# Zero packets of 14 KiB instead of 8 KiB beside the loads and stores of an attention backward kernel

## The chip, the cores and the metric

One core of one Trainium2 chip runs the whole program. The metric is the device time of one execution in microseconds, lower is better. Most executions of a kernel lie within 0.3%, but some runs of the kernel before lie near 800 us (791.42 to 800.26 over 20 runs), so medians and the ratios below differ by a few tenths of a per cent. In what follows PE is the matrix engine, DVE the vector engine and ACT the scalar engine; SBUF is the main memory on the chip, PSUM the one that receives the sums of the PE.

## The reference

One decoder step for two sequences and its gradients: layer norm, attention of 32 query heads (8 key/value heads, 128 wide) over the last 4,096 of 32,768 cached positions, a GeGLU feed-forward block, and the gradients of everything, bf16.

```python
W = min(4096, max(256, Sk // 4))                       # 4096 of 32768
k = jnp.repeat(k_cache[:, :, Sk - W:, :], rep, axis=1)  # v likewise
p = softmax(q k^T * Dh ** -0.5)
h = x + (p v) @ wo ;  h2 = h + (gelu(ln(h) @ w_gate) * (ln(h) @ w_up)) @ w_down
# outputs: h2 and the gradients of x, k_cache, v_cache, wq, wo, w_gate, w_up, w_down
```

The gradients of the two caches are full size. Outside the window they are zero, so 32 regions of 7.34 MB, 235 MB in all, are only zeros to be written. The rest is 49 MB read and 47 MB written.

## The kernel before

Zeros are written by GpSimd DMAs that read a small row of zero bytes again and again and cast each byte to four: a 2 KiB source row gives an 8 KiB packet. The loads and stores go through SyncE's queue. In the profile, q0 is the zeros and q1 the loads and stores.

```python
ZE = 2048
zt = const.tile([P, ZE], U8)                     # zero bytes
ZPK = Z * DH // 2 // ZE                          # 896 packets in a region
ZERO_PARTS = {i: ((4, 1), (15, 2), (2, 2), (15, 42), (12, 3), (P, 1), (16, 4)) for i in (30,)}
def zero_cast(i):                                # (rows, packets per row)
    dst, done = zero_regions[i].bitcast(F32), 0
    for rows, n in ZERO_PARTS.get(i, ((P, ZPK // P),)):
        src = zt[0:rows * (P // rows):P // rows, :]
        nc.gpsimd.dma_start(out=dst[done * ZE:(done + rows * n) * ZE]..., in_=src.unsqueeze(1).to_broadcast([rows, n, ZE]))
        done += rows * n
# ... all 32 are issued at the start and run, in order, whenever the DMA engines have room
```

Region 30 is cut so that transfers of 15 rows leave one DMA engine out. The computation is a chain: attention of batch 0, its middle part, score gradients, the same for batch 1, weight gradients, and a last stage of four jobs that write 8.4 MB of dK or dV each.

```python
def softmax(g):                                  # cut
    ef = stA.tile([P, NJ, REP], F32, tag="ef", name="ef", bufs=1)
    nc.vector.tensor_tensor(out=ef[:], in0=S[:], in1=negm..., op=ALU.add)
    nc.scalar.activation(out=ef[:], in_=ef[:], func=ACT.Exp)
    # ... three DVE reads of ef: ee, eT, lsum

for n, (b, what) in enumerate(jobs):             # last stage, cut
    rhs_bd = nxt
    for gq in range(2):
        # 16 x (2 matmuls, 2 evacuations) into two staging buffers of 16 KiB
        for a in range(2):
            for b2 in range(2):
                nc.sync.dma_start(out=dst_v[:, b, gq * 4 + a * 2 + b2, :, :], in_=sts[a][:, b2, :, :])   # 1 MiB
        if gq == 0 and n + 1 < len(jobs):
            nxt = bd_of(n + 1)                   # its scratch row lies inside staging buffer 1
```

Of the kernel before, what the change touches and what calls it, by code (L numbers as in the profile page):

```python
# [7 lines left out]
BF16 = mybir.dt.bfloat16  # L8
F32 = mybir.dt.float32
U8 = mybir.dt.uint8  # L10
U32 = mybir.dt.uint32
ACT = mybir.ActivationFunctionType
ALU = mybir.AluOpType
AX = mybir.AxisListType
PSUM = bass.MemoryType.PSUM

P = 128
B, D = 2, 512
HQ, HKV, REP, DH = 32, 8, 4, 128
W = 4096  # L20
NJ = W // P
# [6 lines left out]
NOR = (HQ * DH) // P  # L28
SCALE = DH ** -0.5
# [39 lines left out]
def kernel(ctx, tc, A_x, A_k_cache, A_v_cache, A_wq, A_wo, B_x, B_w_gate, B_w_up, B_w_down, grad_out,  # L69
                out_0, out_1, out_2, out_3, out_4, out_5, out_6, out_7, out_8):  # L70
    nc = tc.nc
# [4 lines left out]
    small = ctx.enter_context(tc.tile_pool(name="small", bufs=1))  # L76
# [12 lines left out]
    def evac(out, in_):  # L89
        if evac_i[0] % 2 == 0:  # L90
            nc.vector.tensor_copy(out=out, in_=in_)  # L91
        else:
            nc.scalar.copy(out=out, in_=in_)  # L93
        evac_i[0] += 1
# [3 lines left out]
    dKv = out_2[:, :, Z:, :].rearrange("b g (p j) d -> p b g j d", p=P)  # L98
    dVv = out_3[:, :, Z:, :].rearrange("b g (p j) d -> p b g j d", p=P)

    ZE = 2048
    zt = const.tile([P, ZE], U8)
    zero_regions = [o[b, g, 0:Z, :].rearrange("r d -> (r d)") for o in (out_2, out_3) for b in range(B) for g in range(HKV)]

    ZPK = Z * DH // 2 // ZE

    ZERO_PARTS = {i: ((4, 1), (15, 2), (2, 2), (15, 42), (12, 3), (P, 1), (16, 4)) for i in (30,)}

    def zero_cast(i):
        dst, done = zero_regions[i].bitcast(F32), 0  # L110
        for rows, n in ZERO_PARTS.get(i, ((P, ZPK // P),)):
            src = zt[0:rows * (P // rows):P // rows, :]
            nc.gpsimd.dma_start(out=dst[done * ZE:(done + rows * n) * ZE].rearrange("(p k e) -> p k e", p=rows, k=n),  # L113
                                in_=src.unsqueeze(1).to_broadcast([rows, n, ZE]))
            done += rows * n
# [23 lines left out]
    def load_v(b, g):  # L139
        Vt[b, g] = at(OFF_V + g * 8 * KIB, [P, NJ, DH], BF16, f"V{b}_{g}")  # L140
        nc.sync.dma_start(out=Vt[b, g][:], in_=Vv[:, b, g, :, :])
# [140 lines left out]
    rLb = small.tile([P, HQ], F32)  # L282
    rl = small.tile([P, 1], F32)
    dqT_bf = small.tile([P, NBH], BF16)
    dqT_hb = small.tile([P, HQ, B], BF16)
    dact = small.tile([P, NFR * B], F32)
    M_sb = at(OFF_M, [P, HQ, DH], BF16, "M")
    E = [at(OFF_E[b], [P, 8, 4, HQ], BF16, f"e{b}") for b in range(B)]
# [3 lines left out]
    def prefetch(b, g):  # L292
        if b == 0:
            if g == 0:
# [3 lines left out]
                for i in range(1, 4):  # L298
                    load_k(0, i)
                    load_v(0, i)  # L300
                nc.gpsimd.tensor_scalar(out=zt[:], in0=wq_sb[:, 0, 0:ZE // 2].bitcast(U8),
                                        scalar1=0, scalar2=None, op0=ALU.mult)
# [31 lines left out]
    def attention(b):  # L334
        with tc.tile_pool(name="ps_KT", bufs=2, space=PSUM) as ps_KT, \
# [41 lines left out]
            def softmax(g):  # L377
                S = S_ps.pop(g)
                mx = stA.tile([P, REP], F32, tag="mx", name="mx")
                nc.vector.reduce_max(out=mx[:], in_=S[:].rearrange("p j h -> p h j"), axis=AX.X)  # L380
                mT_ps = ps_A.tile([REP, P], F32, tag="st", name="mT_ps")
                nc.tensor.transpose(out=mT_ps[:], in_=mx[:], identity=ident_f32[:])
                mT = stA.tile([REP, 1], F32, tag="mT", name="mT")
                nc.vector.reduce_max(out=mT[:], in_=mT_ps[:], axis=AX.X)
                md = stA.tile([REP, REP], F32, tag="md", name="md")
                nc.vector.tensor_scalar(out=md[:], in0=ident_f32[0:REP, 0:REP], scalar1=mT[:, 0:1], scalar2=-1.0,
                                        op0=ALU.mult, op1=ALU.mult)
                negm_ps = ps_A.tile([P, REP], F32, tag="st", name="negm_ps")
                nc.tensor.matmul(out=negm_ps[:], lhsT=ones_f32[0:REP, 0:1].to_broadcast([REP, P]), rhs=md[:], start=True, stop=True)
                negm = stA.tile([P, REP], F32, tag="negm", name="negm")  # L390
                nc.vector.tensor_copy(out=negm[:], in_=negm_ps[:])
                ef = stA.tile([P, NJ, REP], F32, tag="ef", name="ef", bufs=1)
                ee = stA.tile([P, NJ, REP, 2], BF16, tag="ee", name="ee")
                nc.vector.tensor_tensor(out=ef[:], in0=S[:], in1=negm[:].unsqueeze(1).to_broadcast([P, NJ, REP]), op=ALU.add)
                nc.scalar.activation(out=ef[:], in_=ef[:], func=ACT.Exp)
                nc.vector.tensor_copy(out=ee[:], in_=ef[:].unsqueeze(3).to_broadcast([P, NJ, REP, 2]))
                Ef[g] = ee
                nc.vector.tensor_copy(out=eT[:].rearrange("p j a q -> p a j q")[:, :, :, g * REP:(g + 1) * REP],
                                      in_=ef[:].rearrange("p (a j) i -> p a j i", a=4))
                nc.vector.reduce_sum(out=lsum[:, 0, g * REP:(g + 1) * REP], in_=ef[:].rearrange("p j h -> p h j"), axis=AX.X)  # L400
# [102 lines left out]
    def middle(b):  # L503
        h0 = b * HQ
        with tc.tile_pool(name="ps_W", bufs=2, space=PSUM) as ps_W, \
             tc.tile_pool(name="ps_B", bufs=1, space=PSUM) as ps_B:
            attn_ps = ps_B.tile([B, D], F32)
            nc.tensor.matmul(out=attn_ps[:], lhsT=ident_bf[32:32 + B, 32:32 + B], rhs=x_32, start=True, stop=False)
            o_sel = at(OFF_KT + 3 * KIB, [P, HQ, 4], BF16, f"o_sel{b}")
# [67 lines left out]
            dhT = transpose_rows(ps_B.tile([P, NDR, B], BF16, tag="sm", name="psT_dh"), dh_bf, f"dh{b}", strided=False, p0=64)  # L577

            dO2_ps = ps_B.tile([P, NOR, B], F32, tag="da", name="dO2_ps")
            dO2 = small.tile([P, NOR], F32, name=f"dO2_{b}", tag="dO2")  # L580
            NPE = 16
            dhB_ps = ps_B.tile([P, D], F32, tag="gu", name="dhB_ps")
            nc.tensor.matmul(out=dhB_ps[:], lhsT=ident_bf[64:64 + B, 64 + b:65 + b].to_broadcast([B, P]), rhs=dh_bf, start=True, stop=True)
# [28 lines left out]
            dqM_ps = ps_B.tile([P, HQ], F32, tag="gu", name="dqM_ps")  # L612
            for q in range(HQ):
                nc.tensor.matmul(out=dqM_ps[:, q:q + 1], lhsT=M_sb[:, q, :], rhs=dOT_bf[:, h0 + q:h0 + q + 1], start=True, stop=True)
            dq_f32 = small.tile([P, HQ], F32, name=f"dq_f32_{b}", tag="dq_f32")
            nc.vector.tensor_tensor(out=dq_f32[:], in0=dqM_ps[:], in1=rLb[:], op=ALU.mult)
            nc.vector.tensor_tensor(out=dq_f32[:], in0=dq_f32[:], in1=pkT[:], op=ALU.subtract)
            nc.vector.tensor_scalar(out=dqT_bf[:, h0:h0 + HQ], in0=dq_f32[:], scalar1=SCALE, scalar2=None, op0=ALU.mult)
            nc.scalar.activation(out=dqT_hb[:, :, b], in_=dq_f32[:], func=ACT.Copy, scale=SCALE)
            if b == 1:  # L620
                ffn_ps = ps_B.tile([B, D], F32, tag="tmp", name="ffn_ps")
                for k in range(NFR):
# [61 lines left out]
    with tc.tile_pool(name="ps_G", bufs=2, space=PSUM) as ps_G:  # L684
# [36 lines left out]
        for (r0, nr) in ((0, 14), (14, 14), (28, 4)):  # L721
            add_group([D] * nr, lambda k, r0=r0: Ro_flat[:, (r0 + k)::NOR], lambda k: DH_bf[:],
                      lambda st, r0=r0, nr=nr: nc.sync.dma_start(out=gwo_v[:, r0:r0 + nr, :],
                                                                 in_=st[:, :nr * D].rearrange("p (a n) -> p a n", n=D)))
# [34 lines left out]
    with tc.tile_pool(name="ps_W2", bufs=2, space=PSUM) as ps_W, \  # L759
         tc.tile_pool(name="ps_G4", bufs=2, space=PSUM) as ps_G, \  # L760
         tc.tile_pool(name="ps_Q", bufs=1, space=PSUM) as ps_Q:
        dq_ps = ps_Q.tile([NBH, DH], BF16, tag="x")
        nc.tensor.transpose(out=dq_ps[:], in_=dqT_bf[:], identity=ident_bf[:])
        dq_bhd = at(OFF_BHD, [NBH, DH], BF16, "dq_bhd")
        nc.vector.tensor_copy(out=dq_bhd[:], in_=dq_ps[:])
        build_R(dq_bhd)
        d_ln1_ps = ps_Q.tile([B, NDR, P], F32)

        def use_q(h, wqT_h):
            nc.tensor.matmul(out=d_ln1_ps[:].rearrange("b a p -> b (a p)"), lhsT=dqT_hb[:, h, :],  # L770
                             rhs=wqT_h[:].rearrange("d a p -> d (a p)"), start=(h == 0), stop=(h == HQ - 1))
        pipelined(HQ, lambda h: tblock(ps_W, lambda r: wq_sb[:, r, h * DH:(h + 1) * DH]), use_q, depth=2)
        ln1 = at(OFF_R1, [B, D], F32, "ln1")
        nc.vector.tensor_scalar(out=ln1[:], in0=x_bf[:], scalar1=mv1[:, 0:1], scalar2=rstd1[:, 0:1],
                                op0=ALU.subtract, op1=ALU.mult)
        nc.vector.tensor_copy(out=ln2_bf[:], in_=ln1[:])
        dx = at(OFF_FROW, [B, D], F32, "dx")
        ln_bwd(d_ln1_ps[:].rearrange("b a p -> b p a"), ln1[:], rstd1, dh[:], "1", dx, at(OFF_FROW + 2 * KIB, [B, D], F32, "tmp"))
        nc.vector.tensor_copy(out=dh_bf, in_=dx[:])
        nc.sync.dma_start(out=out_1.rearrange("b s d -> (b s) d"), in_=dh_bf)  # L780

        L_ps = ps_Q.tile([NBH, D], F32, tag="x")
        nc.tensor.matmul(out=L_ps[:], lhsT=selB, rhs=ln2_bf[:], start=True, stop=True)
        L_bf = at(OFF_L, [NBH, D], BF16, "L")
        nc.vector.tensor_copy(out=L_bf[:], in_=L_ps[:])
        gwq_v = out_4.rearrange("(p r) n -> p r n", r=NDR)
        for r in range(NDR):
            st = at(OFF_WQ + r * 8 * KIB, [P, HQ * DH], BF16, "gq")
            for c4 in range(4):
                ps = ps_G.tile([P, 1024], F32, tag="ps_g", name="ps_gq")  # L790
                for q in range(2):
                    col0 = c4 * 1024 + q * 512
                    nc.tensor.matmul(out=ps[:, q * 512:(q + 1) * 512], lhsT=L_bf[:, r::NDR],  # L793
                                     rhs=Ro_flat[:, col0:col0 + 512], start=True, stop=True)
                evac(st[:, c4 * 1024:(c4 + 1) * 1024], ps[:])
            nc.sync.dma_start(out=gwq_v[:, r, :], in_=st[:])
# [63 lines left out]
```

## Time and profile before

| | before |
|---|---|
| time, median of 20 runs | 792.5 us |
| profiled span | 790.7 us |
| PE, DVE, ACT busy | 72%, 60%, 36% |
| DMA moved | 332.4 MB, 420 GB/s over the span |
| end of attention of batch 1 | 398.7 us |
| last zero packet | 768.5 us |
| R: the fourth job's operand can be built | 750.6 us |

The page cuts the span into 40 slices; a row of 40 rates tells at once whether DMA ever rests. A kernel with one resource that never rests is read from the bytes; only where the row sags does the chain of waits set the time. The moments in the table are starts of single instructions in the trace. "Last zero packet" is by the trace's own zero point; with the packet records lined up by their last end it is 769.8.

### The profile page before, as it was taken

Reading aid. Unit: us, or ns where it says so; the run is one execution under the profiler, and the core shown is the slowest. Engines: PE = TensorE matmul, PEld = TensorE weight load, DVE = VectorE, ACT = ScalarE, POOL = GpSimd, SP = SyncE. Lnnn points to the kernel's source line nnn. Section 1 sums busy time; section 2 is a strip of 40 time slices with the busy share of each in tenths; the row PEclk is TensorE's granted clock in tenths of the full one; section 3 lists DMA queues with packets and bytes.
Section 4 is the critical chain, followed back from the end, with each engine's and each line's share of the span. In section 5 each row is a group of like instructions: output and inputs, shape, how many; then the busy total and the mean of one; then the engine's idle time right before and its main releaser. Section 6 shows DMA issues by size and latency. Waiting matters only on the chain. (4 is left out here: it accounts for less than half of the span.)

```text
span 790.7 us, 12452 instructions
## 1 busy us (share of the span) xinstructions
PE 569.7 (72%) x5096; PEld 303.4 (38%) x5096; DVE 473.8 (60%) x1161; ACT 281.0 (36%) x406; POOL 40.6 (5%) x58
## 2 busy tenths in 40 slices
PE   3899998787687989840937968989697842783072
PEld 3656564445565555420515444534242210220020
DVE  2599999127533989760731386765636953993093
ACT  1434330134345333100201343644444540683062
POOL 4300000000000000000000000000000000000000
PEclk9799999867698999885867868965587685897586
DMA  8999999999999999999999999999999999999998
GB/s 366 418 418 422 419 426 427 423 429 428 427 421 420 425 425 423 426 424 431 427 430 429 428 426 428 428 423 428 434 421 430 423 420 422 424 420 422 422 377 362
DMA packets 40986, 332.44 MB, mean 420 GB/s; under 512 B 2000, under 2 KB 2016, under 8 KB 2144
## 3 DMA queue, kind: packets, MB, share of 16 engines
q0 software_dynamic: 29376, 234.88, 77.7%
q1 hardware_dynamic: 11540, 96.75, 48.9%
q8 instruction: 40, 0.66, 0.3%
q14 instruction: 18, 0.15, 0.0%
q10 hardware_dynamic: 12, 0.01, 0.0%
HBM read 49.30 MB, written 282.33 MB: 419 GB/s over the span
## 5 line engine op out<-in xcount | busy, mean ns | idle before, releaser
L408 DVE TENSOR_TENSOR mem<-mem,ee 128x512 bf16<-128x512 bf16 x512 | 180.9, 416 | 39.9 <-PE M_ps L419 39.9
L419 PE MATMUL M_ps<-mem 128*128 128x512 bf16 x512 | 141.8, 395 | 6.5 <-DVE mem L408 6.2
L93 ACT CAST mem<-ps_g 128x512 bf16<-128x512 f32 x128 | 74.3, 587 | 86.1 <-PE ps_g L822 80.7
L822 PE MATMUL ps_g<-mem 128*128 128x512 bf16 x256 | 82.5, 417 | 20.1 <-DVE mem L91 13.7
L366 ACT COPY mem<-KT_ps 128x1024 bf16<-128x1024 bf16 x64 | 63.1, 1013 | 82.2 <-PE KT_ps L364 77.4
L91 DVE CAST mem<-ps_g 128x512 bf16<-128x512 f32 x128 | 82.6, 688 | 7.1 <-ACT mem L93 3.5
L364 PE MATMUL KT_ps<-ident_bf,mem 128*128 128x128 bf16 x512 | 46.3, 235 | 30.5 <-DMA mem<-in_A_k_cache_dram 25.6
L113 POOL DMA_DIRECT2D out_dram<-zt x38 | 32.5, 998 | 670.7 <-DMA out_dram<-zt 670.4
L419 PEld LDWEIGHTS <-mem 128*128 128x128 bf16 x512 | 44.0, 100 | 49.7 <-issue 16.3
L240 PE MATMUL ps_tb<-ident_bf,mem 128*128 128x128 bf16 x480 | 56.3, 251 | 9.3 <-ACT mem L244 2.7
L822 PEld LDWEIGHTS <-mem 128*128 128x128 bf16 x256 | 25.9, 103 | 76.5 <-issue 56.9
L93 ACT COPY mem<-ps_tb 128x512 bf16<-128x512 bf16 x44 | 25.8, 586 | 72.5 <-PE ps_tb L240 67.7
L240 PEld LDWEIGHTS <-mem 128*128 128x128 bf16 x480 | 37.5, 128 | 34.9 <-issue 30.8
L364 PEld LDWEIGHTS <-mem 128*128 128x128 bf16 x512 | 35.0, 105 | 36.2 <-DMA mem<-in_A_k_cache_dram 26.2
L642 PE MATMUL VT_ps<-ident_bf,mem 128*128 128x128 bf16 x512 | 46.8, 239 | 2.5 <-ACT mem L93 1.1
L651 PE MATMUL dP_ps<-mem 128*128 128x512 bf16 x128 | 44.5, 437 | 4.4 <-ACT mem L93 4.4
L642 PEld LDWEIGHTS <-mem 128*128 128x128 bf16 x512 | 36.6, 107 | 28.0 <-issue 20.7
L91 DVE COPY mem<-ps_tb 128x512 bf16<-128x512 bf16 x44 | 18.7, 424 | 42.1 <-PE ps_tb L240 40.7
L93 ACT COPY mem<-VT_ps 128x1024 bf16<-128x1024 bf16 x31 | 31.7, 1022 | 33.9 <-PE VT_ps L642 32.8
L713 PE MATMUL ps_gr<-mem 2*128 2x512 bf16 (+1 forms) x78 | 33.7, 498 | 11.8 <-DVE mem L733 7.4
L91 DVE CAST mem<-ps_gr 128x512 bf16<-128x512 f32 (+1 forms) x38 | 24.7, 655 | 27.8 <-PE ps_gr L713 27.8
L261 PE MATMUL ps_rows<-ident_bf,mem 128*128 128x128 bf16 x4 | 1.1, 288 | 55.2 <-DVE mem L260 55.2
(242 smaller groups left out, 629.2 us busy)
## 6 DMA issues: line engine op xcount, KB each, us to landing
out_dram<-zt POOLq DMA_DIRECT2D x31, 7168.0 KB, 165.0
out_dram<-mem SPq DMA_DIRECT2D x36, 1024.0 KB, 26.7
mem<-in_A_k_cache_dram SPq DMA_DIRECT2D x16, 1024.0 KB, 23.4
mem<-in_A_v_cache_dram SPq DMA_DIRECT2D x16, 1024.0 KB, 23.5
out_dram<-mem SPq DMA_DIRECT2D x5, 1792.0 KB, 18.7
out_dram<-zt POOLq DMA_DIRECT2D x1, 5040.0 KB, 130.0
mem<-in_A_wq_dram SPq DMA_DIRECT2D x1, 4096.0 KB
mem<-in_A_wo_dram SPq DMA_DIRECT2D x1, 4096.0 KB, 31.3
```

Source lines behind the costliest of these rows:

```text
L91: nc.vector.tensor_copy(out=out, in_=in_)
L93: nc.scalar.copy(out=out, in_=in_)
L113: nc.gpsimd.dma_start(out=dst[done * ZE:(done + rows * n) * ZE].rearrange("(p k e) -> p k e", p=rows, k=n), in_=src.unsqueeze(1).to_broadc ...
L240: nc.tensor.transpose(out=ps[:, a, :], in_=src_block(a), identity=ident_bf[:])
L364: nc.tensor.transpose(out=KT_ps[:, jj, :], in_=Kt[b, g][:, u * 8 + jj, :], identity=ident_bf[:])
L366: nc.scalar.copy(out=KT[:], in_=KT_ps[:])
L408: nc.vector.tensor_tensor(out=pk[:, :, i, :].rearrange("p j (d t) -> p j d t", t=2), in0=Kb[:, j0:j0 + pk_j, :].rearrange("p j (d t) -> p ...
L419: nc.tensor.matmul(out=M_ps[:], lhsT=Vt[b, g][:, j, :], rhs=pk[:, jj, :, :].rearrange("p i d -> p (i d)"), start=(j == 0), stop=(j == NJ - 1))
L642: nc.tensor.transpose(out=VT_ps[:, jj, :], in_=Vt[b, g][:, a * 8 + jj, :], identity=ident_bf[:])
L651: nc.tensor.matmul(out=dP_ps[:, c, :], lhsT=dOpad[:, w0:w0 + P], rhs=VT[:, c * 4:(c + 1) * 4, :].rearrange("d a k -> d (a k)"), start=(i = ...
L713: nc.tensor.matmul(out=ps[:, :n], lhsT=lhsT_fn(k), rhs=rhs_fn(k), start=True, stop=True)
L822: nc.tensor.matmul(out=ps[:, a2, :], lhsT=lhs_bf[:, jp * P:(jp + 1) * P], rhs=rhs_bd[:, ap * 2 + a2, gq * 4:(gq + 1) * 4, :].rearrange("q ...
```

## The change

The intent: larger zero packets, so fewer of them, and less cost per byte. A 14 KiB packet needs a zero row of 3.5 KiB; the room is found by doing the softmax in place in PSUM, by dropping a second copy of dq, and by a pool that reuses memory for two small tiles. The transfers that leave out an engine have even counts.

```diff
-    ZE = 2048
+    ZE = 3584
-    ZERO_PARTS = {i: ((4, 1), (15, 2), (2, 2), (15, 42), (12, 3), (P, 1), (16, 4)) for i in (30,)}
+    ZERO_PARTS = {i: ((4, 1), (15, 2), (2, 2), (15, 26), (12, 3), (16, 3)) for i in (30,)}
-    dqT_hb = small.tile([P, HQ, B], BF16)
-                ef = stA.tile([P, NJ, REP], F32, tag="ef", name="ef", bufs=1)
+                ef = S
-            dO2 = small.tile(...)            # and dq_f32
+            dO2 = mid.tile(...)              # a pool opened in middle()
-            nc.scalar.activation(out=dqT_hb[:, :, b], in_=dq_f32[:], func=ACT.Copy, scale=SCALE)
-            nc.tensor.matmul(..., lhsT=dqT_hb[:, h, :], ...)
+            nc.tensor.matmul(..., lhsT=dqT_bf[:, h::HQ], ...)
```

More of the change, by code (lines that the diff above doesn't have):

```diff
@@ L505, in middle @@
         with tc.tile_pool(name="ps_W", bufs=2, space=PSUM) as ps_W, \
-             tc.tile_pool(name="ps_B", bufs=1, space=PSUM) as ps_B:
+             tc.tile_pool(name="ps_B", bufs=1, space=PSUM) as ps_B, \
+             tc.tile_pool(name="mid", bufs=1) as mid:
             attn_ps = ps_B.tile([B, D], F32)
@@ L579, in middle @@
             dO2_ps = ps_B.tile([P, NOR, B], F32, tag="da", name="dO2_ps")
-            dO2 = small.tile([P, NOR], F32, name=f"dO2_{b}", tag="dO2")
+            dO2 = mid.tile([P, NOR], F32, name=f"dO2_{b}", tag="dO2")
             NPE = 16
@@ L614, in middle @@
                 nc.tensor.matmul(out=dqM_ps[:, q:q + 1], lhsT=M_sb[:, q, :], rhs=dOT_bf[:, h0 + q:h0 + q + 1], start=True, stop=True)
-            dq_f32 = small.tile([P, HQ], F32, name=f"dq_f32_{b}", tag="dq_f32")
+            dq_f32 = mid.tile([P, HQ], F32, name=f"dq_f32_{b}", tag="dq_f32")
             nc.vector.tensor_tensor(out=dq_f32[:], in0=dqM_ps[:], in1=rLb[:], op=ALU.mult)
@@ L769, in use_q @@
         def use_q(h, wqT_h):
-            nc.tensor.matmul(out=d_ln1_ps[:].rearrange("b a p -> b (a p)"), lhsT=dqT_hb[:, h, :],
+            nc.tensor.matmul(out=d_ln1_ps[:].rearrange("b a p -> b (a p)"), lhsT=dqT_bf[:, h::HQ],
                              rhs=wqT_h[:].rearrange("d a p -> d (a p)"), start=(h == 0), stop=(h == HQ - 1))
```

## The prediction

> **What bounds the kernel now.** I read the page's slices first. They show a full DMA system and compute engines that are not full (PE 72%, DVE 60% of the span).
>
> ```profile
> DMA  8999999999999999999999999999999999999998
> GB/s 366 418 418 422 419 426 427 423 429 428 427 421 420 425 425 423 426 424 431 427 430 429 428 426 428 428 423 428 434 421 430 423 420 422 424 420 422 422 377 362
> q0 software_dynamic: 29376, 234.88, 77.7%
> q1 hardware_dynamic: 11540, 96.75, 48.9%
> ```
>
> The reader is to see that from the second slice to the 38th the rate stays between 418 and 434 GB/s, and falls only in the first and the last two. Of 332 MB, 234.88 MB are zeros on q0: 28,672 packets of 8 KiB, plus 704 completion writes. If the zeros always fill what the loads and stores (q1) leave, the time is bytes divided by rate, plus the ends where DMA is not full. So I looked at how fast each mixture runs (stretches by window: PE, PEld, DVE, ACT, POOL, clock, DMA share, GB/s) and at what holds the end (the chain of waits from 600 us on: start, us, what).
>
> ```profile
> 226.00:266.00 40.00, 34.36 (x429) 23.18 (x428) 18.72 (x51) 18.69 (x21) 0.90 (x1) 0.91 1.25 419
> 170.00:220.00 50.00, 38.76 (x378) 27.04 (x378) 26.72 (x69) 20.42 (x34) 2.71 (x3) 0.75 1.15 428
> 694.00:750.00 56.00, 21.31 (x72) 6.78 (x71) 24.13 (x38) 21.58 (x37) 0.93 (x1) 0.74 1.14 421
> 772.00:786.00 14.00, 4.18 (x15) 1.24 (x13) 6.04 (x10) 4.76 (x9) 0.00 (x0) 0.73 0.97 406
> ```
>
> ```profile
> 633.79 30.73 DMA out_dram<-mem
> ...
> 682.02 28.88 DMA out_dram<-mem
> 710.92 39.57 DMA out_dram<-mem
> 750.54 0.04 issue
> 750.58 0.21 DVE mem L260
> ```
>
> 170 to 220 us is zeros alone (428 GB/s), 226 to 266 zeros beside K/V loads (419), 694 to 750 zeros beside the dK/dV stores (421), 772 to 786 stores alone (406). In the chain the last stage waits for stores to land, twice for long. The DVE copy at L260 writes a scratch row that lies inside the second staging buffer, so the operand of the last of four dK/dV jobs can't be built before the third job's first four stores (1 MiB each) have landed, at 750.6 us. I call that moment R. From R to the end are 40.1 us of DVE/ACT evacuation and one last drain, whatever the zeros do.
>
> From the packet records: q0 has moved 205.3 MB by 632 us, 26.2 MB more up to R and 3.4 MB after R, its last packet at 769.8 us. q1 moves 23.8 MB from 632 us to R and 12.0 MB after it. So R itself is bound by DMA, the last 40 us by the engines.
>
> **What the Trainium skill says.** (1) "DMA: Bandwidth & Descriptors", Where 436 GB/s comes from: 16 ports x 32 B x 850 MHz = 435.2 GB/s is the ceiling, and about 358 the HBM share. The trace agrees with the first (428 measured) and contradicts the second (HBM traffic at 419 all through). (2) Same page, Queues, rings and completion order: each engine goes round-robin between its queues at packet granularity. The trace agrees: beside 8 KiB rows q0:q1 is 219:198 GB/s (227 to 266 us), beside 14 KiB rows (w_down, 414 to 419 us) 155:270, a ratio of 1.74 where the sizes have 1.75. (3) Same page, Why a DMA increments its semaphore by 16: software transfers over k < 16 engines take consecutive engines from a round-robin cursor. Then 15 rows leave one engine out; no view here names engines. (4) "VectorE: DVE Perf Modes", Why PSUM operands drop a tier: an fp32 operand in PSUM gets no fast mode. No softmax operation is shown from PSUM alone here; the add from PSUM at L394 takes 285 ns for 128 elements, the cast from SBUF at L398 219.
>
> **The change, part by part.**
>
> *Fewer, larger zero packets.* 28,672 packets become 32 x 512 = 16,384, each 14,336 B; bytes are unchanged. Per engine 1,792 become 1,024. Cost per packet: zeros alone at 427 GB/s (packet records, 170 to 220 us) is 26.7 GB/s per engine, 307 ns for 8,192 B, against 301 at the ceiling: 6 ns over. With 14,336 B: 527 + 6 = 533 ns, or 430.5 GB/s, +0.8%. Zeros are alone for 349 us between 26 and 750 us: 2.8 us saved. For the mixture I have a measured stand-in, 14 KiB rows on q1 beside 8 KiB zeros: 425 GB/s (w_up at 144 to 148, w_down at 414 to 419 us), against 415 to 417 for K/V loads and 421 for stores of 8 KiB. Assuming that which side is larger does not matter: 158 us of loads x 2.0% = 3.2 us, 125 us of stores x 0.95% = 1.2 us, 90 us of other mixtures x 0.5% = 0.4 us. Sum: 7.6 us of DMA time saved up to R.
>
> *The shares move.* Beside 8 KiB rows the zeros get 14/22 of the rate, 270 GB/s instead of 219, and q1 155 instead of 200. A 1 MiB load or store takes 6.8 us of its queue instead of 5.3. Attention needs 2.1 MB per head and about 13.4 us (K loads issued at 45.5, 59.1, 72.5, 85.5 us), that is 157 GB/s: just kept up, with three heads already in SBUF. In the last stage the first landing wait (664.6 us) moves some 12 us later. This delays compute, not R: zeros left at 632 us, 29.6 minus 2 MB thanks to the better rate, are gone 27.6/0.270 = 102 us later, at 734 us instead of 769.8. Until then q1 has moved 15.8 of its 23.8 MB; the other 8.0 MB go alone at about 417 GB/s (first packets of the 1 MiB stores after 768 us are 2.5 us apart) in 19 us, so R is near 753. Counted the other way: the 3.4 MB that were written after R now come before it, 3.4/0.425 = +8.1 us, +0.3 us for running stores alone at 417 instead of mixed, against -7.6: R +0.8 us. The two ways agree within 2 us.
>
> *After R.* Nothing competes with the last stores. Before, the four stores issued at 719 to 730 us landed only at 768; now they are gone by R + 11. The last 4.2 MB still go out after the last evacuation: 1 us saved at most.
>
> *Zero tile.* The POOL operation that makes it took 5,372 ns for 2,048 elements; 3,584 need 9.4 us. Zeros start 4 us later (first packet 25.1 us before), while q1 has a backlog of loads and keeps the engines full: 0.
>
> *Softmax in PSUM, 2 columns by stride, pool for two small tiles.* 16 softmaxes x three DVE reads (L396 312, L398 219, L400 374 ns), at most 0.1 us each more: under 5 us of DVE in attention, part of it on the compute path, none at R. Two ACT copies go. One score tile lives longer, but its next writer is most of a head away: 0. This part only makes the room.
>
> *Balance.* The engine left out gets 7 packets of region 30 where most get 47 (40 x 8 KiB = 328 KB less); after, 7 against 31 (24 x 14 KiB = 344 KB). Even counts change no bytes: 0.
>
> Sum: +0.8 at R, -1 after it, -1 because engines drift apart less once the zeros are gone (4 us between the store's last data packet by order and its release at R, 1.6 at the first wait): about -1 to -2 us on 793.4. I say 791.5.
>
> **Rivals.** *The rate gain is realised in full:* DMA time 8 to 13 us shorter and the end follows, about 782 to 785. For it: 37 full slices. Against it: the 40 us after R, where the rate already sags to 377 and 362; zeros that finish early leave that tail emptier, not shorter. *Starved loads and stores:* q1 at 155 GB/s becomes the bound. Isolated transfers already wait: 10.6 to 12.8 us from issue to first packet while zeros run alone, and the PE stood 25.3 us for the last K tile of batch 1. If that wait is a fixed number of zero packets (32 to 40) it grows by 7 us each, and with a lost head or two R would turn compute-bound: 800 to 812. Against it: the third job's stores need to be ready only near 740 us in my count and would be at 720, a slack near 20 us. If the wait is a fixed amount of buffered source bytes (2 KiB per packet, now 3.5), it stays as it is. *14 KiB casts are cut internally* into 8 and 6 KiB pieces: no rate gain, R +8, near 800.
>
> **Range and chances.** The two large terms, +8.1 and -7.6 us, cancel, and each may be off by half: +-5 us. Single runs of before already spread from 791.4 to 799.8. So 784 to 800 should hold it 8 times in 10. Over 2% faster (below 777.5) needs all of the rate gain and a shorter tail: 0.03. Over 2% slower (above 809) needs starvation to break the slack: 0.04.
>
> **What would show it.** q0 with about 16,384 large packets; zeros alone at 430 to 432 GB/s; mixed with K/V near 425 and shares 270:155; last zero packet near 735 us; the L260 wait for stores in the middle near 42 us instead of 30.8; R near 750 to 753; last slices without zeros still near 370. Wrong if: the mixed rate stays at 417 to 421 (no gain per packet), PE waits for K or V several times (starvation), or the end comes less than 36 us after R.

## The result, and the profile after

The changed kernel takes 799.55 us (798.83 to 800.1, 10 runs), the kernel before 792.5. The ratio is 1.0071 with a 95% interval of 1.0044 to 1.0097. Ratios are the mean time of one kernel's runs over that of the other's of the same rounds, so not quite the ratio of the medians. It is slower, by less than 2%.

The page of the changed kernel, slices and queues:

```profile
DMA  8999999999999999999999999999999999999948
GB/s 367 419 420 423 422 430 422 429 426 431 428 427 423 422 426 426 426 424 432 431 429 430 431 430 431 427 429 427 427 431 428 432 425 423 425 425 410 408 198 350
q0 software_dynamic: 17056, 234.88, 72.8%
```

The rates are on the whole a little higher up to the 36th slice; then come 410, 408 and a hole of 198 GB/s. The packets are 16,384 as intended (the rest of the 17,056 are completion writes).

The last part of each span, by window (us, then busy time of PE, PEld, DVE, ACT and POOL, granted clock, DMA share, GB/s). Before:

```profile
600.00:720.00 120.00, 75.20 (x223) 23.40 (x222) 88.56 (x131) 62.76 (x103) 2.38 (x4) 0.76 1.18 423
750.00:790.70 40.70, 20.81 (x65) 6.33 (x65) 25.85 (x38) 18.63 (x32) 0.00 (x0) 0.75 0.95 370
```

After:

```profile
600.00:720.00 120.00, 68.47 (x284) 24.05 (x284) 66.77 (x103) 46.37 (x74) 2.49 (x4) 0.73 1.23 426
720.00:757.00 37.00, 27.21 (x88) 8.70 (x86) 29.37 (x46) 25.60 (x44) 0.00 (x0) 0.87 0.99 408
757.00:797.70 40.70, 21.18 (x65) 6.50 (x65) 26.15 (x38) 18.53 (x32) 0.00 (x0) 0.75 0.67 277
```

The last 40.7 us hold the same compute in both kernels (PE 20.8 and 21.2 us, the same 65 matmuls), but DMA moves 370 GB/s in them before and 277 after. No zeros were left to fill the gaps between the stores: they ended at 727.4 us instead of 768.5.

The chain of waits of the changed kernel (start, us, what):

```profile
655.16 41.80 DMA out_dram<-mem
...
697.06 0.21 DVE mem L260
...
729.77 10.49 DMA out_dram<-mem
...
742.07 15.03 DMA out_dram<-mem
...
757.19 0.21 DVE mem L260
```

The first landing wait is 41.8 us (30.7 before), a second of 10.5 us lies between, and the last ends at 757.2: R is 6.6 us later. From R to the end it is 40.5 us, 40.1 before.

What the PE waited for (us in total, times, longest). Before, then after:

```profile
PE KT_ps L364 <- DMA mem<-in_A_k_cache_dram: 25.6, 2, 25.3
```

```profile
PE KT_ps L363 <- DMA mem<-in_A_k_cache_dram: 46.7, 5, 29.5
```

The K tiles come later, as the zeros beside them take 276 GB/s instead of 229. Attention of batch 1 ends at 417.8 us, 19.1 us late.

Two tables from the packet records settle where the bytes were. Bytes moved by a given time, in MB, zeros in brackets:

| us | before | after |
|---|---|---|
| 600 | 254.0 (194.2) | 254.8 (197.0) |
| 720 | 304.7 (225.7) | 306.0 (233.8) |
| 750 | 317.3 (231.6) | 318.3 (234.9) |
| 770 | 324.9 (234.9) | 324.1 (234.9) |
| 780 | 328.9 | 326.3 |

From 30 to 720 us, how long each mixture ran and at what rate (packets of q0 and q1 alone, in steps of 2 us; steps in which a transfer starts or ends, 48 and 68 us, are left out):

| mixture | before: us, GB/s (q0, q1) | after: us, GB/s (q0, q1) |
|---|---|---|
| zeros alone | 346, 427.9 | 296, 429.7 |
| beside 8 KiB loads | 148, 417.0 (229, 188) | 188, 420.8 (276, 144) |
| beside 8 KiB stores | 94, 420.7 (218, 202) | 76, 424.7 (265, 160) |
| beside rows of 14 or 32 KiB | 54, 421.5 (144, 277) | 62, 424.2 (199, 226) |
| mean of all steps | 423.8 | 425.9 |

Every mixture is faster, by 0.4 to 0.95%. The mean gains 0.5%, which is 1.3 MB or 3.1 us at 720 us. By 770 us the kernel before has overtaken it.

### The profile page after: what moved, and what is told of

The parts are those of the page before. It is cut to its first block, busy times and chain, and to the rows that moved or that the text cites. A ratio compares the mean times of both kernels' runs of the same rounds, so it can differ in the third digit from the quotient of the medians.

```text
span 797.7 us, 12454 instructions
## 1 busy us (share of the span) xinstructions
PE 568.3 (71%) x5096; PEld 299.3 (38%) x5096; DVE 475.9 (60%) x1161; ACT 277.8 (35%) x404; POOL 37.9 (5%) x57
## 3 DMA queue, kind: packets, MB, share of 16 engines
q0 software_dynamic: 17056, 234.88, 72.8%
## 5 line engine op out<-in xcount | busy, mean ns | idle before, releaser
L363 PE MATMUL KT_ps<-ident_bf,mem 128*128 128x128 bf16 x512 | 44.1, 231 | 48.8 <-DMA mem<-in_A_k_cache_dram 46.7
L113 POOL DMA_DIRECT2D out_dram<-zt x37 | 25.9, 778 | 616.8 <-DMA out_dram<-zt 596.0
L91 DVE COPY mem<-ps_tb 128x512 bf16<-128x512 bf16 x44 | 18.7, 424 | 42.0 <-PE ps_tb L240 40.7
L91 DVE COPY mem<-VT_ps 128x1024 bf16<-128x1024 bf16 x33 | 23.1, 701 | 27.5 <-PE VT_ps L641 26.9
```

Source lines behind the costliest of these rows:

```text
L91: nc.vector.tensor_copy(out=out, in_=in_)
L363: nc.tensor.transpose(out=KT_ps[:, jj, :], in_=Kt[b, g][:, u * 8 + jj, :], identity=ident_bf[:])
```

## The experiments

Most runs share one edit: the changed kernel with the packet size chosen per region, each size with its own split of region 30.

```diff
+    PARTS = {1024: ..., 2048: <the split of before>, 3584: <the split of after>}   # 1024: the 2048 one, counts doubled
+    ZES = [...]                              # 32 sizes, one per region
     def zero_cast(i):
+        ze = ZES[i]; zpk = Z * DH // 2 // ze
-        src = zt[0:rows * (P // rows):P // rows, :]
+        src = zt[0:rows * (P // rows):P // rows, 0:ze]
```

At a glance, all in us. The moments are of the profiled execution; the median is of the timed ones, 1 to 2.5 us above the span. "End of attention 1" is the start of the last group of M_ps matmuls of batch 1.

| run | end of attention 1 | last zero | R | span | median | ratio to before |
|---|---|---|---|---|---|---|
| before | 398.7 | 768.5 | 750.6 | 790.7 | 792.5 | |
| after | 417.8 | 727.4 | 757.2 | 797.7 | 799.55 | 1.0071 |
| e1_room_only | 401.7 | 768.9 | 754.6 | 794.4 | 795.55 | 1.0054 |
| e2_early8 | 401.4 | 744.0 | 757.7 | 798.3 | 799.78 | 1.0093 |
| e3_late8 | 419.0 | 753.6 | 759.3 | 799.7 | 801.47 | 1.0115 |
| e4_odd | 417.9 | 727.6 | 758.1 | 798.9 | 800.22 | 1.0096 |
| e5_hold | 415.9 | 771.8 | 751.7 | 795.5 | 798.01 | 1.0076 |
| e6_early8_hold | 401.1 | 768.2 | 748.2 | 792.4 | 793.74 | 1.0021 |
| e7_tail4 | 402.0 | 775.5 | 739.9 | 791.0 | 793.02 | 1.0012 |
| e8_14_tail4 | 417.6 | 768.7 | 753.9 | 794.5 | 796.06 | 1.0055 |
| e9_hold_mended | 406.9 | 767.4 | 748.0 | 788.8 | 790.37 | 0.9945 |
| e10_sbuf_softmax | 397.0 | 769.0 | 749.7 | 790.2 | 792.34 | 0.9974 |
| e11_no_skip | 417.2 | 744.0 | 769.1 | 810.2 | 811.54 | 1.0211 |
| e12_split_zeros | 384.4 | 775.7 | 739.0 | 791.8 | 793.69 | 1.002 |

A moment of a single profile scatters: e6_early8_hold and e9_hold_mended are the same program up to the last stage, and their attention ends at 401.1 and 406.9 us. So no difference of a few us in that column says much alone.

The first call put the obvious reading of the traces to the test: theory S, that late K tiles cost the time, against P (softmax in PSUM) and T (the last stage alone).

### The room without the packets

```diff
+    ZES = [2048] * 32          # ZE = 2048
```

> The changed kernel with zero packets of 8 KiB again and the split of region 30 as it was: only the room-making part is left (softmax in PSUM, strided columns, second pool). Theory S (starvation: beside 14 KiB zero packets the loads get 143 to 146 GB/s instead of 198, K tiles come late in attention, and compute is 19 us late by the end of attention of batch 1): 791 to 794 us, attention of batch 1 ends near 399 us, one long K wait near 25 us, ratio to before 0.997 to 1.003. Rival P (softmax in PSUM slows the heads): about 799 us with attention ending near 418. Rival T (only the last stage suffers from the new shares): 791 to 794 too, so this run tells P from S and T.

Measured 795.55 us, R 754.6. It fits none of the three exactly: the room alone costs 3 us, a part of P. The stores of the last stage are first issued at 635.8 us instead of 632.4, and R moves by 4.0. Here, as before, the zeros outlast R, so q1 has its half of the rate until R, and R seems to move with the start of the stores (one profile of each).

### 8 KiB through attention, 14 KiB after it, and the mirror image

```diff
+    ZES = [2048] * 14 + [3584] * 18
```

> The changed kernel with 8 KiB packets in zero regions 0 to 13 (until about 384 us, both attention stages) and 14 KiB in the rest. S: attention of batch 1 ends at 399 to 401 us, first landing wait of the last stage still near 42 us, zeros gone near 730 us, R (the operand of the fourth job is released) 750 to 753 and bound by DMA, time 790 to 794 us. P and T: as the changed kernel, 799 to 800 us.

Measured 799.78 us. S falls. Attention ended at 401.4 us as S said, 16 us earlier than in the changed kernel, and the time did not move. The last windows show why:

```profile
720.00:757.00 37.00, 15.44 (x53) 4.87 (x51) 18.51 (x29) 15.76 (x28) 0.00 (x0) 0.80 1.06 425
757.00:798.00 41.00, 21.18 (x65) 6.49 (x65) 26.16 (x38) 18.54 (x32) 0.00 (x0) 0.75 0.65 270
```

DMA runs at 425 GB/s right up to R at 757.7 us, so R is bound by bytes, and then the last 41 us have only 270 GB/s left to move. The 8 KiB packets also give up a part of the better rate: 305.6 MB have moved at 720 us, where the changed kernel has 306.0. P and T foretold this time too; the next run speaks against T, and the first spoke against P as the whole cause.

```diff
+    ZES = [3584] * 14 + [2048] * 18
```

> The mirror image: 14 KiB packets in zero regions 0 to 13, 8 KiB in the rest. S: attention of batch 1 ends near 418 us as in the changed kernel, first landing wait near 31 us instead of 42, zeros end near 740 us instead of 726, R near 753 to 756 and time 793 to 797 us: the late compute is partly made good, as stores get their old share. T: 791 to 793. P: 799 to 800.

Measured 801.47 us, outside all three ranges. Attention ended at 419.0 us as S said and R came at 759.3. The zeros ended at 753.6, still before R.

### Odd counts

```diff
-    ((4, 1), (15, 2), (2, 2), (15, 26), (12, 3), (16, 3))
+    ((4, 1), (15, 3), (2, 2), (15, 25), (12, 3), (16, 3))
```

> The changed kernel with region 30 cut as 15 rows x 3 and 15 rows x 25 packets instead of 2 and 26: odd counts in both transfers that leave out an engine, the same sums per engine within one packet. Nothing in the traces so far speaks for the evenness: within 0.3% of the changed kernel, 798 to 801 us. If odd counts cost something, slower by 1% or more, and the zeros end later on some engines.

Measured 800.22 us, 0.1% from the changed kernel's median and with overlapping intervals. Evenness shows no effect here.

### Zeros held back until R

From the first four runs came theory D: where all zeros are written before R, R is the moment when all bytes but the last 12.6 MB have moved. It holds over the runs, with about 11 MB left in place of 12.6: bytes moved at R are 321.3 MB in the changed kernel, 321.5 in e2_early8, about 322 in e3_late8 and 321.3 in e4_odd, at 757 to 759 us. In the kernel before they are 317.6, since some 3 MB of zeros follow R. D says that moving zeros behind R brings the time back.

```diff
+    hz = at(OFF_KT, [P, 2048], U8, "hz")                  # free in the last stage
+    ZES = [3584] * 31 + [2048]                            # e6 and e9: [2048] * 14 + [3584] * 17 + [2048]
+    # region 31 in two transfers of 3 and 4 packets per partition; the second (4.2 MB) waits:
                     nxt = bd_of(n + 1)
+                    if n + 1 == 3:
+                        nc.gpsimd.tensor_scalar(out=hz[:], in0=<2 KiB of the new operand>, scalar1=0, scalar2=None, op0=ALU.mult)
+                        zero_cast(31, hold=True)
```

> The first four runs contradict theory S: with 8 KiB packets through both attention stages attention ends at 401 us instead of 418, and the time is the same 799.8. New theory D: when the zeros are all written before R, R is the moment at which every byte but the last 12.6 MB of stores has moved, whatever compute did before; the time is R + 40. This run: the changed kernel with 4.2 MB of the last zero region held back until the operand of the fourth job exists, so that they are written after R. D: 4.2 MB less before R would be 9.9 us earlier, but the third job's stores are issued only at 740 to 742 us here and land 10 to 12 us later, so R near 752 to 753 instead of 757 and 793 to 796 us. If late compute (S) sets R alone: R 757, 799 to 800 us.

Measured 798.01 us, so the time is outside what D said (793 to 796), though R is close: 751.7 us, where D had 752 to 753. From R to the end it took 43.8 us.

> Held-back zeros as in the run before, and 8 KiB packets in zero regions 0 to 13, so that compute comes early as in the second run. D: R falls from 757.7 (second run) by about 9 us to 748 to 750, time 788 to 791 us, below the kernel before or equal to it. S: holding back changes nothing beyond the second run, 799 us.

Measured 793.74 us, outside the 788 to 791 of D. Again R is where D put it, 748.2 us, and again the part after R is longer, 44.2 us. Between the two, the early compute is worth 3.5 us of R: in e5_hold the third job's stores are issued at 741 us, so with the zeros out of the way late compute does bind. The chain of e6_early8_hold after R has this:

```profile
750.19 5.81 DVE mem L278 x2
```

Those two steps of building the operand take 2.4 us in the other runs. The GpSimd operation that writes the 2 KiB row runs at the same time. So the row was made early, and only 16 bytes per partition were written at R:

```diff
+        nc.gpsimd.memset(hz[:], 0)                        # at the start of the stage
-                        nc.gpsimd.tensor_scalar(out=hz[:], ...)
+                        nc.gpsimd.tensor_scalar(out=hz[:, 0:16], ...)
```

> The sixth run again (8 KiB in regions 0 to 13, 14 KiB after, 4.2 MB of zeros held back until R), but the zero row for the held-back part is made early, and only 16 bytes per partition are written at R. There R fell to 748.2 us as theory D said, but R to the end took 44.2 us instead of 40, with the DVE building the fourth operand at 5.8 us for two steps instead of 2.4 beside the long GpSimd operation. Expected: R 747 to 749, R to end 40 to 41, profile span 787 to 790, median 789 to 791.5, ratio to before 0.996 to 0.999. If the 4 us belong to the zeros after R themselves (contention): 793 to 794 again.

Measured 790.37 us (790.32 to 790.66), ratio 0.9945. R is 748.0, and from R to the end 40.8 us. The two steps and the last window:

```profile
749.87 2.37 DVE mem L278 x2
```

```profile
748.00:788.80 40.80, 20.74 (x65) 6.33 (x65) 25.32 (x38) 18.53 (x32) 1.84 (x2) 0.76 0.98 391
```

The last 41 us move 391 GB/s instead of 270. Against the changed kernel R is 9.2 us earlier (757.2 to 748.0), and so is the median (799.55 to 790.37). They were run at other times. This version beats both kernels: the slowest of its six runs (790.66) lies below the fastest of the eleven of the kernel before (791.59). The gain over the kernel before is small: 0.1 to 1.0% by the interval, whose rounds hold three runs of the kernel before near 800 us, and 0.3% by the medians (792.64 to 790.37).

### Smaller packets in the last stage

Another way to keep zeros for the end: 4 KiB packets in the last four regions, so that stores get about two thirds of the rate.

```diff
+    ZES = [2048] * 28 + [1024] * 4
```

> 8 KiB packets in zero regions 0 to 27, 4 KiB in the last four (softmax in PSUM as in the first run). Stores get about 2/3 of the rate in the last stage instead of 1/2. D: zeros are no longer all written before R, the third job's stores land far earlier: R 715 to 730, zeros end only at 780 to 786, the end is then bound by the last bytes: 787 to 792 us; mixed rate in the last stage 412 to 416 GB/s instead of 421. If R + 40 held here too: about 760 to 770 us, which the bytes do not allow.

Measured 793.02 us, 2.5 us better than e1_room_only, its nearest relative. R is 739.9 us, earlier than in any run so far, though not the 715 to 730 expected; the zeros end at 775.5. The end no longer follows R by 40 us but by 51: DMA binds it, not the computing. The mixture with stores ran at 417 GB/s (690 to 740 us).

```diff
+    ZES = [3584] * 28 + [1024] * 4
```

> 14 KiB packets in zero regions 0 to 27, 4 KiB in the last four: the better rate early, the stores' share late. D: despite compute being 20 us late (attention ends near 418 us), zeros outlast R, and the end is bound by bytes: 786 to 791 us, 1 to 2 us below the run before. S: late compute shows at the end, 799 us or more.

Measured 796.06 us, between the two ranges. The last 14 KiB packet ends at 639 us, so the stores have their larger share from the start, as in e7_tail4 (first landing wait 22.5 us). But compute is late: the stores begin at 654.0 us instead of 637.8, and R is 753.9 instead of 739.9, with zeros left until 768.7. So late compute does cost where zeros outlast R.

### The softmax alone, and the split alone

```diff
-                ef = S
+                ef = stA.tile([P, NJ, REP], F32, tag="ef", name="ef", bufs=1)     # on e1_room_only
```

> The first run (8 KiB everywhere, 795.5 us) with the softmax back in SBUF: left of the change are the strided columns and the second pool. If the softmax in PSUM delayed attention by the 3 us: attention of batch 1 ends near 399 us, R 750 to 751, 791.5 to 793 us, ratio 0.998 to 1.002. If the pool or the columns did it: 795 us again.

Measured 792.34 us (the kernel before: 792.64; the ratio of 0.9974 again has its runs near 800 in it): the kernel before again, R 749.7, attention of batch 1 ending at 397.0 us. So the softmax in PSUM is what cost e1_room_only its 3 us. The DVE operations do not add up to it: two casts are slower, the reduction is faster, together some 80 ns more per softmax, 1.3 us over 16. The groups of e1_room_only (busy us, mean ns):

```profile
L398 DVE CAST ee<-S_ps 128x256 bf16<-128x256 f32 x16 | 6.7, 421 | 0.7 <-ACT S_ps L397 0.5
L402 DVE TENSOR_REDUCE lsum<-S_ps 128x4 f32<-128x128 f32 x16 | 4.5, 283 | 0.0
```

The cast is 109 ns slower than in the kernel before (312), a second cast of the same tile (L400) 63 ns slower (282 and 219), the reduction 91 ns faster (374). In e1_room_only the first heads are 14.4 and 13.7 us apart where the kernel before has 13.5 and 13.4, and one head takes 5.7 us more, of which 2.4 are a wait for a K tile. What lengthens them, the score tile that is held longer or the order of instructions, was not tried.

```diff
-    ZERO_PARTS = {i: (...) for i in (30,)}       # on the changed kernel
+    region 30 in one transfer of 128 rows x 4 packets
```

> The changed kernel with region 30 written as one transfer over all 16 engines, no engine left out. The engine that was spared gets 344 KB more, 13 us of its work, but the zeros end at 727 us, 30 us before R, and the stores queue behind them on each engine. D: R waits for the slowest engine, 3 to 10 us later than 757, 802 to 810 us. If the split does not matter at all: 799 to 800.5 us.

Measured 811.54 us, 12 us slower than the changed kernel. The zeros end at 744.0 us instead of 727.4 and R is 769.1 instead of 757.2. D's sign is right, and it is larger than expected: the cost is about the 13 us of one engine's work that the split spares it. The windows show that engine:

```profile
766.00:776.00 10.00, 3.96 (x9) 1.07 (x10) 5.96 (x8) 1.52 (x3) 0.00 (x0) 0.50 0.06 27
```

For 10 us DMA moves 27 GB/s at a busy share of 0.06, one of 16 engines, while the rest have nothing to do. Which engine it is, and why it is slower, the trace doesn't say.

### Shorter zero transfers

On the kernel before: each region in four transfers instead of one.

```diff
-        for rows, n in ZERO_PARTS.get(i, ((P, ZPK // P),)):
+        for rows, n in ZERO_PARTS.get(i, ((P, 2), (P, 2), (P, 2), (P, 1))):
```

> The kernel before with every zero region but the split one written as four transfers (2, 2, 2 and 1 packets of 8 KiB per partition) instead of one of 7. In both traces the last K tile's data end some 15 us before the PE is released, and the 4-byte completion writes end in the same moment as those of the zero transfer then running. If a completion write with nothing behind it waits for the end of the zero transfer, the lag falls from 15 us to at most 5 and the PE's wait for that K tile from 25 us to 13 to 17; compute is then some 10 us early at the end of attention (387 to 391 us), the stores start earlier, more zeros are left after R, and the time is 788 to 792 us. If the lag has another cause, the wait stays at 25 us and the time at 792.

The mechanism holds: the PE's wait for the last K tile is 15.8 us, and no completion write in that stretch lags over 4.6 us.

```profile
PE KT_ps L364 <- DMA mem<-in_A_k_cache_dram: 15.8, 1, 15.8
```

Attention ends at 384.4 us, 14 us earlier, and R is 739.0, but the time is 793.69 us, no better, and outside the 788 to 792 expected. DMA is never idle up to 780 us and has moved 0.4 MB less at 720 us than the kernel before. This is the plainest sign that the kernel before is bound by DMA: 14 us less of waiting gains nothing. It is not the bytes alone, though. The two stretches before the end, with all computing done:

```profile
770.00:782.00 12.00, 0.00 (x0) 0.00 (x0) 0.00 (x0) 0.00 (x0) 0.00 (x0) 0.50 1.03 421
782.00:788.00 6.00, 0.00 (x0) 0.00 (x0) 0.00 (x0) 0.00 (x0) 0.00 (x0) 0.50 0.66 277
```

At 277 GB/s and a share of 0.66 about ten of 16 engines still have work (an estimate, from the 27 GB/s of one engine in e11_no_skip). e7_tail4 shows the same 277. Whether a more even spread of the last bytes gains time was not tried.

## Why the prediction was right or wrong

The time, 799.55 us, lies in the range (784 to 800) by half a microsecond, which is luck: two of the ten runs lie above 800. "Within 2%" was given 0.93. The point, 791.5, is 8 us low. Two of its three signs of being wrong appeared, at least in part: beside loads the rate was 420.8 GB/s (it had named 417 to 421), and the PE waited for K five times. The last two slices came at 198 and 350, where "near 370" was said. By its own steps:

- **Shares: right.** Beside 8 KiB rows zeros took 276 and 265 GB/s and q1 144 and 160, where 270 and 155 were said; the first landing wait is 41.8 us, where 42 was said; the zeros ended at 727 us (734).
- **R as a matter of bytes: right as a mechanism, wrong in size.** R came at 757, where 750 to 753 was said. e2_early8 and e6_early8_hold show the mechanism, which was its main idea: 16 us of earlier compute left R where it was (757.7; the lower rate early, 0.4 MB or 1 us, works against it), 4.2 MB of zeros put behind R moved it by 9.5 us (757.7 to 748.2).
- **The term +8.1 us, zeros that no longer run after R: right.** The windows of 370 and 277 GB/s are this term; e9_hold_mended takes it back. Measured it is 3.2 MB, 7.5 us.
- **The term -7.6 us, the better rate: this is the step that failed.** It measured 3.1 us. Zeros alone gained 0.4% (429.7 GB/s) where 0.8 was said (430.5, an estimate from the ceiling that it cites; its own 533 ns give 430.4), beside loads 0.9% where 2.0 was said, beside stores 0.95% as said. The stand-in (14 KiB rows on q1 beside 8 KiB zeros) does not carry over to 14 KiB zeros beside 8 KiB rows. And the times were held fixed, though the change itself lengthens the slow mixture: with 144 instead of 188 GB/s the loads run 188 us instead of 148, at 421 GB/s instead of the 430 of zeros alone.
- **-1 us after R and -1 us for engines that drift less: did not come.** From R to the end is 40.5 us against 40.1.
- **"Attention just kept up" and "slack near 20 us": half right.** Two K tiles came 8 us late each and attention ended 19 us late; this used up the slack, so that job 3's stores were issued at 740 to 742 us. It cost R a little even while the bytes bound it. Stores alone ran at 425 GB/s while their queue was full, more than the 417 counted; but on some engines the queue ran short before the stores issued at 729.4, 740.3 and 751.4 us, and from 727.4 us to R the mean is 405, where e2_early8, with early stores, has 426. That is about 1.3 us (an estimate: 19 GB/s short of 424 over 29.8 us). With the zeros out of the way, e5_hold shows late compute as the next bound, 3.5 us behind.
- **Softmax in PSUM, "none at R": wrong where zeros outlast R.** There it costs 3 us (e1_room_only against e10_sbuf_softmax). In the changed kernel no run separates it; all the lateness of compute together cost about 1.3 us there.
- **The wait of isolated transfers**, left open between a number of packets and an amount of source bytes: the first packet still comes 10.7 to 11.5 us after issue with packets 1.75 times as large, so it is not a number of packets.

The changed kernel's stores alone, with a full queue and around the gap at 740 us:

```profile
731.00:740.00 9.00, 7.91 (x28) 2.58 (x27) 8.73 (x14) 7.72 (x14) 0.00 (x0) 1.00 1.02 425
739.50:742.00 2.50, 2.23 (x9) 0.76 (x8) 2.39 (x5) 2.09 (x5) 0.00 (x0) 1.00 0.86 360
```

The sum of +7.5, -3.1 and +1.3 explains 5.7 of the 6.6 us by which R moved. Of the rivals, the full rate gain did not come, and starvation came but cost R little.

## What to carry to other kernels

When DMA is full and background writes fill its gaps, ask not only how fast they run but when they run out: what is left for the last, compute-bound stretch is worth its full time, and a change that finishes the background earlier loses it. Larger background packets also take a larger share from the foreground, and holding back just the amount that the tail can carry was worth more (9 us, from 799.6 to 790.4, together with smaller packets early) than the packet size (3 us of rate). Before counting a rate gain over fixed times per mixture, ask how the change moves the times.

## What the Trainium skill lacked or had wrong

- "DMA: Bandwidth & Descriptors", Where 436 GB/s comes from: for HBM traffic it says that about 358 GB/s per core binds. Only the note under the table of measured rates, on the same page, limits this to two cores that stream at once. With one core at work, as here, 418 to 434 GB/s run for 37 of 40 slices; so the prediction's "contradicts" is true of that section read alone.
- The same page does not say what larger packets gain between 8 and 14 KiB, or what two queues with rows of different size reach together: from 8 to 14 KiB zeros alone gain 427.9 to 429.7 GB/s, beside 8 KiB loads 417.0 to 420.8.
- The same page, Latency and other measured facts, gives some 0.6 us to the first byte of a SyncE transfer. With idle engines 1.0 us was seen; beside zeros alone it was 10.6 to 11.5 us, and 10.7 to 11.5 with 14 KiB packets (the prediction's 10.6 to 12.8 had the alignment error in it).
- The same page, Queues, rings and completion order, says that a semaphore write lands only after every earlier write of its engine, across queues; it does not say how long that can take. Here a transfer's 4-byte completion writes, with nothing behind them in their queue, ended in the same moment (within 0.01 us for most) as those of the zero transfer in the other queue, up to 16.8 us after they began; with zero transfers a quarter as long the lag was at most 4.6 us, and the PE's wait fell from 25.3 to 15.8 us.
- "VectorE: DVE Perf Modes", Why PSUM operands drop a tier: the cast became slower from PSUM (312 to 421 ns) but the reduction faster (374 to 283 ns), and the page does not have the second.
- "DMA: Bandwidth & Descriptors" says which engines are usually slower, with no cost: leaving no engine out cost 12 us (799.55 to 811.54).
